# Attention and two feed-forward layers on one core: one ring of banks for the sums of the later blocks, two rings for their attention, scores due two pairs at a time

## The chip, the cores and the metric

The kernel runs on one core of a Trainium2 chip. The metric is device time in microseconds (us) of the whole kernel, as the median of the runs. The engines are named as the profile names them: PE (matrix products; PEld is its weight load), DVE (vector), ACT (scalar), POOL (GpSimd) and SP, whose queue starts most transfers.

## What is computed

```python
def reference(**kwargs):
    attn_out = _attn_ref(**attn_kwargs)      # q, k, v: (4, 8, 576, 64), causal window of 128, ALiBi bias
    x = attn_out.transpose(0, 2, 1, 3).reshape(B * S, H * D)   # 2304 tokens x 512
    x = _moe_ref(x=x, **moe_kwargs)          # h = x @ w_in (512 x 2048); g = gate(h); g @ w_out
    return _moe2_ref(x=x, **moe2_kwargs)

# _attn_ref
scores = scale * q @ k.T;  mask = (rel >= 0) & (rel < window)
scores = np.where(mask, scores + bias, -1e9)
attn = exp(scores - max) / (sum + 1e-09);  out = attn @ v
# _moe_ref
g = np.where(h >= 1, h, np.where(h <= -1, 0.0, (h + 1) ** 2 / 4))
# _moe2_ref: tokens with x @ w_skip > 0 also pass through one of 8 experts; the others are returned as they are
```

## The kernel before

The 2304 tokens are cut into 9 blocks of 256 (18 tiles of 128). A block needs attention for 4 pairs of heads and then 8 feed-forward steps, each over 256 of the 2048 hidden columns. fp32 operands of the feed-forward layers are split into a high and a low part, and three products stand for one, so a step is 24 matmuls of the first layer (L528, 128x256) and 12 of the second (L559, 128x512).

**Attention of one pair** (`pair`, L311 on). Load of q, k and v (L324, L327); q scaled (L334 on ACT, L336 on POOL); scores on PE in 64-row tiles, for the first blocks whole (L347: 4 instructions, 8 records) and for the later ones in halves on 64x64 tiles (L359: 8 instructions, 16 records); on DVE the merge of the halves (L376; whole: L370) and bias, row minimum and write to `sn` (L382); exp on ACT (L388); reciprocal of the row sums on DVE (L397, L398); normalisation (L416 on ACT, L419 on POOL); transposes on PE (L424); the copy to `pts` (L293); two masked selections into `ab` on POOL (L307); the product with v on PE in 128x64 tiles (L446: 6 instructions, 12 records); copy and rest into `xT` (L293, L302). `PLAN["whole"]` says how many blocks take whole scores.

**A feed-forward step** (`tile_ff`): first product (L528), `u` and its square on ACT (L540, L545), the gate on DVE (L550), high part on ACT (L293, `g<-h`), low part on DVE (L302, `g<-h,g`), second product (L559) into two accumulators of 128x512. The first three blocks run interleaved while the 32 weight tiles are being prepared (`weight`: ACT L474 and L293, DVE L480, L494, L499, L302); later blocks run one after the other. When a block is done, `evacuate` copies both sums out (ACT L293, `stage<-r`) and reduces them for the second layer's choice (DVE L574).

**PSUM.** There are eight banks in four rings of two: `h` for the first product, and `r0`, `r1`, `r2`, which `att` (scores, transposes, products with v) and `sums` (accumulators) hand out: block 0 sums in r0, block 1 in r1, block 2 in r2, later blocks in r2 and r1 by turns; attention takes r2 for the first three blocks and r0 afterwards.

**What sets the order.** No loop runs on the device: a planner (`Plan.order`) lays the pieces out on all five engines from costs, due times and buffer rings, and every engine executes its row in that order. `PLAN` holds its constants (`lead`: how far ahead of a block's first step its attention is due, and `spread`: how far apart the four pairs are), `ENGINES` the engines that each operation may choose from. Where the plan leaves PE idle early on, `run` inserts filler matmuls (L603) that no result depends on.

Of the kernel before, what the change touches and what calls it, by code (L numbers as in the profile page):

```python
# [22 lines left out]
P = 128  # L23
B, H, S, D = 4, 8, 576, 64
NT = B * S
DM = H * D
# [5 lines left out]
NPAIR = H // 2  # L32
# [12 lines left out]

PLAN = dict(base=4.418, d0=10.283, d1=3.632, d3=3, d2=5.432, lag=1, lag2=9, ahead=19.774, lead=22.491, spread=2,
            margin=1.2, slack=0.049, fin=0.449, passes=5, first=3, stick=4.711, zeros=0, whole=2)

ENGINES = dict(norm="AP", wlo="DP", rebias="A", pt="A", whi="A", square="A", scale="AP")

# [47 lines left out]
class Plan:  # L98
# [5 lines left out]
    def add(self, cost, fn, deps=(), new=(), use=(), due=1e9, lag=0.0, port=False,  # L104
            mode=""):
        p = Piece(len(self.pieces), cost, fn, [d for d in deps if d is not None], new, use, due, lag, port, mode)
        self.pieces.append(p)
        return p
# [129 lines left out]
dve = lambda n: n / 960.0 + 0.072  # L238
dve2 = lambda n: n / 1920.0 + 0.072
act = lambda n: n / 1200.0 + 0.108  # L240
actp = lambda n: n / 1200.0 + 0.068
# [4 lines left out]
class Fused:  # L246
# [23 lines left out]


    def bank(self, ring, shape):
        return self.buf(ring, 2, shape, psum=True)

    def att(self, g, shape):
        return self.bank("r2" if g < 3 else "r0", shape)

    def sums(self, g):
        return [self.bank(("r0", "r1", "r2")[g] if g < 3 else ("r2", "r1")[g % 2], [P, DM]) for _ in range(2)]

# [15 lines left out]

    def pick(self, key, **cost):
        return {e: cost[e] for e in ENGINES[key]}

# [12 lines left out]
    def pair(self, g, p, due):  # L312
        add, nc, a = self.plan.add, self.nc, self.a
# [4 lines left out]
        whole = g < PLAN["whole"]  # L318
        qk = self.buf("qkraw", 2, [P, 5, P])
        v = self.buf("vraw", 2, [P, 3, P])  # L320
        hd = slice(2 * p, 2 * p + 2)
        heads = [(odd, slice(64 * odd, 64 * odd + 64)) for odd in range(2)]
# [15 lines left out]

        lq = add(self.pick("scale", A=0.4, P=0.43, D=dve2(256)), scale, [lq], use=[qk], port=True)
        s = [self.att(g, [P, 2, 4, 64]) for _ in heads]  # L340

# [18 lines left out]

        sn = self.buf("sn", 2, [P, 4, P])
        sd = add({"T": (0.87 if g else 0.66) if whole else 0.63 if g else 0.5}, scores, [lq], new=s + [sn], use=[qk], mode="rows")
        st = self.buf("st", 4, [P, 2, 4])
        exps = []
        for odd, o in heads:
# [20 lines left out]
            def exp(e, odd=odd):  # L386
                for x in range(2 * odd, 2 * odd + 2):
# [3 lines left out]
            d = add({"D": dve(128 * (1 + j)) if whole else 2 * dve(64 * (1 + j)) + 0.06}, merge, [sd], use=[s[odd]])  # L391
            d = add({"D": 0.416}, rowmax, [d], new=[] if odd else [st],
                    use=[s[odd], sn, st])
# [8 lines left out]
        for odd, o in heads:  # L402
            pt = self.bank("r1", [P, 2, P]) if g < 2 else self.att(g, [P, 2, P])
            pts = self.buf("pts", 2, [P, 2, P])
# [21 lines left out]
            def before(e, pts=pts, ab=ab):  # L426
                if g == 0:
                    self.select(ab.t[:, 2:3, :], pts.t[:, 1:2, :], False)
                else:
                    self.select(ab.t[:, 0:4:2, :], pts.t, False)  # L430

            d = add(self.pick("norm", A=0.586, D=dve(256), P=0.67), norm, [rs], use=[sn, st], port=True)
            d = self.chain("tr", add({"T": 0.221}, transpose, [d], new=[pt, pts], use=[sn]))
            d = add(self.pick("pt", A=actp(256), D=dve(256)), lambda e, ptv=ptv, pts=pts: self.copy(e, pts.t, ptv()), [d],
                    use=[pt, pts])
            d1 = self.chain("ab", add({"P": pool1(256 if g else 128)}, before, [d], new=[ab], use=[pts]))
            last.append((o, ab, add({"P": pool1(256)}, lambda e, pts=pts, ab=ab: self.select(ab.t[:, 1:4:2, :], pts.t, True),
                                    [d, d1], use=[pts, ab])))
        av = self.att(g, [P, 2, P]) if g else self.bank("r0", [P, 2, P])

# [164 lines left out]
    def run(self):  # L605
# [12 lines left out]
        for g in range(NBLK):  # L618
            for p in range(NPAIR):
                self.pair(g, p, tau[pos[g, 0]] - c["lead"] - (NPAIR - 1 - p) * c["spread"] if g > 2 else 1e9)  # L620
        w = {}
# [215 lines left out]
```

## Time and profile before

| what | value |
|---|---|
| median of 3 runs | 527.0 us (526.81 to 528.45) |
| the profiled execution: device time | 527.1 us |
| its span, first to last instruction | 525.3 us |
| PE busy | 509.4 us, 97% of the span |
| ACT busy | 301.4 us, 57% |
| DVE busy | 277.2 us, 53% |
| POOL busy | 100.7 us, 19% |
| granted PE clock, mean | 0.995 |

Busy time is the time in which the profile shows an instruction on the engine. In a row of a timeline, the first number is the start in us from the span's beginning, the second the time from the first start to the last end; since matmuls overlap, what a group takes from PE is the distance from its start to the start of the next group. A wait in square brackets is idle time just before the group and what ended it.

### The profile page before, as it was taken

Reading aid. Unit: us, or ns where it says so; the run is one execution under the profiler, and the core shown is the slowest. Engines: PE = TensorE matmul, PEld = TensorE weight load, DVE = VectorE, ACT = ScalarE, POOL = GpSimd, SP = SyncE. Lnnn points to the kernel's source line nnn. Section 1 sums busy time; section 2 is a strip of 40 time slices with the busy share of each in tenths; the row PEclk is TensorE's granted clock in tenths of the full one; section 3 lists DMA queues with packets and bytes.
Section 4 is the critical chain, followed back from the end, with each engine's and each line's share of the span. In section 5 each row is a group of like instructions: output and inputs, shape, how many; then the busy total and the mean of one; then the engine's idle time right before and its main releaser. Section 6 shows DMA issues by size and latency. Waiting matters only on the chain.

```text
span 525.3 us, 10059 instructions
## 1 busy us (share of the span) xinstructions
PE 509.4 (97%) x3700; PEld 429.9 (82%) x3702; DVE 277.2 (53%) x844; ACT 301.4 (57%) x784; POOL 100.7 (19%) x244
## 2 busy tenths in 40 slices
PE   7999999999999999999999999999999999999994
PEld 3567898888888898889888988888888988889883
DVE  5989999998365225532555236422653265223221
ACT  6999778777477336643575237633763277433330
POOL 2673000234014200330033002400231013200000
PEclk9999999999999999999999999999999999999997
DMA  8565555553121202120212012210212020101001
GB/s 268 163 231 192 189 178 151 190 172 113 49 90 52 61 1 92 50 61 1 67 52 65 21 49 67 57 32 1 91 52 60 1 92 1 31 0 41 1 0 44
DMA packets 27141, 41.12 MB, mean 78 GB/s; under 512 B 2000, under 2 KB 15952, under 8 KB 27088
## 3 DMA queue, kind: packets, MB, share of 16 engines
q1 hardware_dynamic: 26416, 40.12, 24.2%
q8 instruction: 30, 0.49, 0.4%
q10 hardware_dynamic: 672, 0.33, 0.2%
q14 instruction: 23, 0.19, 0.1%
HBM read 35.72 MB, written 4.72 MB: 77 GB/s over the span
## 4 chain that ended last, share of the span: by engine, by line
PE 76%; DVE 11%; ACT 5%; DMA 3%; issue 2%; POOL 0%; SPq 0%; ACTq 0%; POOLq 0%; DVEq 0%
PE h L528 32%; PE r L559 32%; PE r L446 6%; PE r L359 4%; ACT sn L388 2%; PE r L424 2%; DVE stage L494 2%; DVE wtmp L499 2%; DVE r L376 2%; DMA qkraw<-in_qk 1%; DMA stage<-in_w_in 1%; DMA stage<-in_w_out 1%; DVE stage L480 1%; DVE sn L382 1%; ACT sn L416 1%
## 5 line engine op out<-in xcount | busy, mean ns | idle before, releaser
L528 PE MATMUL h<-xT,wi 128*128 128x256 f32 x1728 | 222.9, 282 | 0.6 <-POOL wi L302 0.4
L528 PEld LDWEIGHTS h<-xT,wi 128*128 128x128 f32 x1728 | 213.6, 188 | 11.7 <-issue 5.2
L559 PE MATMUL r<-wo,g 128*128 128x512 f32 x864 | 219.1, 400 | 0.0
L559 PEld LDWEIGHTS r<-wo,g 128*128 128x128 f32 x864 | 156.0, 188 | 37.7 <-issue 4.4
L550 DVE SCALAR_TENSOR_TENSOR h<-h,u 128x512 f32<-128x512 f32 x72 | 50.3, 698 | 129.3 <-ACT u L545 126.6
L540 ACT ACTIVATE u<-h,half 128x512 f32<-128x512 f32 x72 | 49.4, 686 | 111.1 <-PE h L528 110.5
L419 POOL TENSOR_SCALAR sn<-sn,st 128x128 f32<-128x128 f32 x70 | 27.1, 400 | 237.4 <-ACT u L540 175.7
L388 ACT ACTIVATE sn<-sn,st 128x128 f32<-128x128 f32 x144 | 56.1, 391 | 27.1 <-DVE st L382 27.0
L307 POOL TENSOR_SCALAR_AFFINE_SELECT ab<-pts 128x256 f32<-128x256 f32 (+1 forms) x144 | 56.5, 426 | 53.5 <-ACT pts L293 44.0
L293 ACT ACTIVATE g<-h 128x512 fp32r<-128x512 f32 x72 | 42.8, 594 | 33.1 <-DVE h L550 32.9
L302 DVE TENSOR_TENSOR g<-h,g 128x512 fp32r<-128x512 f32 x72 | 49.6, 689 | 22.2 <-ACT g L293 21.3
L545 ACT ACTIVATE u<-u 128x512 f32<-128x512 f32 x72 | 45.5, 632 | 1.4
L376 DVE COPY_PREDICATED r<-mask,r 64x128 f32<-64x128 uint8 x112 | 33.2, 296 | 15.9 <-PE r L359 12.9
L446 PE MATMUL r<-ab,vraw 128*64 128x128 f32 (+1 forms) x416 | 35.6, 315 | 3.5 <-ACT pts L293 1.7
L446 PEld LDWEIGHTS r<-ab,vraw 128*64 128x64 f32 x416 | 25.2, 136 | 14.6 <-issue 3.8
L382 DVE CUSTOM_DVE_ANT_0 sn<-r,nrel 128x128 f32<-128x128 f32 x144 | 33.3, 286 | 0.8
L574 DVE CUSTOM_DVE_ANT_0 junk<-r,wskip 128x512 f32<-128x512 f32 x18 | 12.4, 691 | 37.1 <-ACT stage L293 36.5
L388 ACT ACTIVATION_READ_ACCUMULATOR sn<-sn,st 128x1 f32 x144 | 27.0, 188 | 0.0
L416 ACT ACTIVATE sn<-sn,st 128x128 f32<-128x128 f32 x74 | 25.4, 394 | 1.7 <-DVE st L398 1.2
L424 PE MATMUL r<-ident,sn 128*128 128x128 f32 x144 | 23.7, 277 | 1.6 <-POOL sn L419 1.2
L474 ACT ACTIVATE wtmp<-stage 128x512 f32<-128x512 f32 x32 | 21.7, 679 | 5.3 <-DVE wi L302 2.2
L359 PE MATMUL r<-qkraw 64*64 64x192 f32 x448 | 24.7, 335 | 0.0
(43 smaller groups left out, 282.1 us busy)
## 6 DMA issues: line engine op xcount, KB each, us to landing
qkraw<-in_qk SPq DMA_DIRECT2D x32, 320.0 KB, 3.0
stage<-in_w_in SPq DMA_DIRECT2D x16, 512.0 KB, 3.6
stage<-in_w_out SPq DMA_DIRECT2D x16, 512.0 KB, 3.7
vraw<-in_v SPq DMA_DIRECT2D x32, 192.0 KB, 2.7
out_x<-stage SPq DMA_DIRECT2D x18, 256.0 KB, 2.0
qkraw<-in_qk SPq DMA_DIRECT2D x4, 256.0 KB, 4.2
vraw<-in_v SPq DMA_DIRECT2D x4, 128.0 KB, 4.2
nrel<-in_nrel ACTq DMA_DIRECT2D x1, 256.0 KB, 3.9
```

The source lines that it names most:

```text
L293: self.nc.scalar.activation(out=out, in_=in_, func=AF.Copy)
L302: eng.tensor_tensor(out=out, in0=in0, in1=in1, op=ALU.subtract)
L307: self.nc.gpsimd.affine_select(out=out, in_=in_, pattern=[[0, n], [sign, P]], compare_op=ALU.is_ge if causal else ALU.is_gt, fill=0.0, base=0,
L359: nc.tensor.matmul(s[odd].t[r, i, 1 - half:4 - half, :], qk.t[o, 3 + i, r], k, start=True, stop=True)
L376: nc.vector.copy_predicated(s.t[r, 1 - j:2, 1 + half, :], self.mask[r, 1 - j:2, r], s.t[r, 1 - j:2, 3 * (1 - half), :])
L388: nc.scalar.activation(out=sn.t[:, x, :], in_=sn.t[:, x, :], func=AF.Exp, scale=-1.0, bias=st.t[:, 0, x:x + 1], accum_out=st.t[:, 1, x:x + 1])
L446: nc.tensor.matmul(av.t[o, out, :], v.t[:, k, o], ab.t[:, m, :], start=not more, stop=True, skip_group_check=more)
L528: nc.tensor.matmul(h.t[:, c, :], w[:, wz, k, :], x.t[:, xz, k].rearrange("p a b -> p (a b)"), start=k == 0 and i == 0, stop=k == NKC - 1 a ...
L540: r = add({"A": 0.167 + 0.213 * n}, lambda e: nc.scalar.activation(out=uv(), in_=hv(), func=AF.Relu, scale=0.5, bias=self.half), [d], new= ...
L545: nc.scalar.activation(out=uv(), in_=uv(), func=AF.Square)
L550: r = add({"D": dve(256 * n)}, lambda e: nc.vector.scalar_tensor_tensor(out=hv(), in0=hv(), scalar=1.0, in1=uv(), op0=ALU.max, op1=ALU.min ...
L559: nc.tensor.matmul(acc[i].t, gt.t[:, gz, c, i * P:(i + 1) * P], self.wo[:, f, wz, :], start=f == 0 and j == 0, stop=f == NF - 1 and j == 2)
```

## The change

The accumulators of every block from block 3 on are taken from ring r1 alone. From block 4 on (`turn=4`) attention uses r0 for pairs 0 and 2 and r2 for pairs 1 and 3. The due time of the pairs comes in twos from block 4 on (`p | 1`). q and k get 4 buffers (2 before), v 3 (2), `sn` 3 (2). Block 2 has whole scores too (`whole=3`). In the later blocks the normalisation may go to DVE as well, the copy to `pts` to DVE or ACT; the first three blocks keep the choices that they had (keys ending in `0`). The low part of the weights is left to DVE alone, and for weight tile 0 one shift moves from DVE to a product on POOL (`zeros=1`). All other constants of the planner are new, and with them the order on every engine.

```diff
-PLAN = dict(base=4.418, d0=10.283, d1=3.632, ..., ahead=19.774, lead=22.491, spread=2, ..., zeros=0, whole=2)
-ENGINES = dict(norm="AP", wlo="DP", rebias="A", pt="A", whi="A", square="A", scale="AP")
+PLAN = dict(base=2.305, d0=10.296, d1=4.965, ..., ahead=15, lead=50.043, spread=7.771, ..., zeros=1, whole=3, turn=4)
+ENGINES = dict(norm="ADP", wlo="D", rebias="A", pt="AD", whi="A", square="A", scale="AP", norm0="AP", pt0="A",
+               scale0="AP")
...
-    def att(self, g, shape):
-        return self.bank("r2" if g < 3 else "r0", shape)
+    def att(self, g, p, shape):
+        return self.bank("r2" if g < 3 or g >= PLAN["turn"] and p % 2 else "r0", shape)
 
     def sums(self, g):
-        return [self.bank(("r0", "r1", "r2")[g] if g < 3 else ("r2", "r1")[g % 2], [P, DM]) for _ in range(2)]
+        return [self.bank(("r0", "r1", "r2")[g] if g < 3 else "r1", [P, DM]) for _ in range(2)]
...
-    def pick(self, key, **cost):
+    def pick(self, key, g=9, **cost):
+        if g < 3:
+            key += "0"
         return {e: cost[e] for e in ENGINES[key]}
...
-        qk = self.buf("qkraw", 2, [P, 5, P])
-        v = self.buf("vraw", 2, [P, 3, P])
+        qk = self.buf("qkraw", 4, [P, 5, P])
+        v = self.buf("vraw", 3, [P, 3, P])
...
-        sn = self.buf("sn", 2, [P, 4, P])
+        sn = self.buf("sn", 3, [P, 4, P])
...
-                self.pair(g, p, tau[pos[g, 0]] - c["lead"] - (NPAIR - 1 - p) * c["spread"] if g > 2 else 1e9)
+                self.pair(g, p, tau[pos[g, 0]] - c["lead"] - (NPAIR - 1 - (p if g < c["turn"] else p | 1)) * c["spread"]
+                          if g > 2 else 1e9)
```

In the order that comes out, PE's lines move by four (L359 is L363, L424 is L428, L446 is L450, L528 is L532, L559 is L563). Counted over the whole order, PE goes to scores 36 times before and 27 times now: the 24 pairs of blocks 3 to 8 had 24 such visits and have 15, since nine times the scores of two pairs stand next to one another, and the four pairs of block 2 have whole scores. It goes to the product with v 21 times before and 26 times now. There are 36 filler matmuls before and 38 now.

**PE, from a pair's last transposes to the products with v, in a later block.** Before (block 5; `r` is a bank of a ring, x12 and x24 are matmuls of the first feed-forward product):

```order
L559 MATMUL r_2599<-wo,g 128x512 x6
L424 MATMUL r_2797<-ident,sn 128x128 x2
L424 MATMUL r_2801<-ident,sn 128x128 x2
L528 MATMUL h<-xT,wi 128x256 x12
L446 MATMUL r_2830<-ab,vraw 64x256 x2
L446 MATMUL r_2830<-ab,vraw 64x128 x4
L446 MATMUL r_2837<-ab,vraw 64x256 x2
L446 MATMUL r_2837<-ab,vraw 64x128 x4
```

Now:

```order
L428 MATMUL r_3185<-ident,sn 128x128 x2
L428 MATMUL r_3190<-ident,sn 128x128 x2
L563 MATMUL r_2712<-wo,g 128x512 x6
L532 MATMUL h<-xT,wi 128x256 x24
L450 MATMUL r_3236<-ab,vraw 64x256 x2
L450 MATMUL r_3236<-ab,vraw 64x128 x4
L450 MATMUL r_3246<-ab,vraw 64x256 x2
L450 MATMUL r_3246<-ab,vraw 64x128 x4
```

Between the transposes and the products that need them stand 12 matmuls of the first layer before, and 6 of the second with 24 of the first now.

**DVE, from the last row minimum of a visit to the low part of g, in a later block.** Before:

```order
L382 ISA st_3991 128x1
L550 SCALAR_TENSOR_TENSOR h_3912<-h_3912,u_3974 128x512
L397 TENSOR_SCALAR st_3991<-st_3991 128x4
L398 RECIPROCAL st_3991<-st_3991 128x4
L302 TENSOR_TENSOR g_4015<-h_3912,g_4015 128x512
```

Now (numbers behind the names tell buffers apart):

```order
L386 ISA st_4006 128x1
L554 SCALAR_TENSOR_TENSOR h_3927<-h_3927,u_4002 128x512
L401 TENSOR_SCALAR st_3992<-st_3992 128x4
L402 RECIPROCAL st_3992<-st_3992 128x4
L415 TENSOR_TENSOR sn_3948<-sn_3948,st_3992 128x256 x2
L401 TENSOR_SCALAR st_4006<-st_4006 128x4
L402 RECIPROCAL st_4006<-st_4006 128x4
L415 TENSOR_TENSOR sn_3959<-sn_3959,st_4006 128x256
L306 TENSOR_TENSOR g_4059<-h_3927,g_4059 128x512
```

Ahead of the first row stand the merges and row minima of one pair before (two rows of x2 merges and 4 minima) and of two pairs now (four rows of x2 and 8 minima); behind the gate, the low part of g now also stands behind two reciprocals and three normalisations.

**ACT, the first instructions of the program after its table load and two transfers.** Before:

```order
L334 ACTIVATE qkraw_110<-qkraw_110,qscale_87 128x256
L334 ACTIVATE qkraw_112<-qkraw_112,qscale_87 128x256
L474 ACTIVATE wtmp_142<-stage_114 128x512
L388 ACTIVATE sn_129,st_139<-sn_129,st_139 128x128 x4
L474 ACTIVATE wtmp_174<-stage_135 128x512
L388 ACTIVATE sn_155,st_167<-sn_155,st_167 128x128 x4
```

Now:

```order
L338 ACTIVATE qkraw_110<-qkraw_110,qscale_87 128x256
L338 ACTIVATE qkraw_112<-qkraw_112,qscale_87 128x256
L338 ACTIVATE qkraw_114<-qkraw_114,qscale_87 128x256
L338 ACTIVATE qkraw_116<-qkraw_116,qscale_87 128x256
L392 ACTIVATE sn_129,st_142<-sn_129,st_142 128x128 x4
L478 ACTIVATE wtmp_169<-stage_118 128x512
L392 ACTIVATE sn_156,st_171<-sn_156,st_171 128x128 x4
```

All four pairs of block 0 are scaled on ACT, the first exps no longer stand behind a weight tile, and on SP's queue four loads of q and k (two before) stand ahead of the first weight tile.

## Rows read from the trace of the kernel before

**Rows 1.** The page's part 1, PE: busy us (share of the span) xinstructions.

```profile
PE 509.4 (97%) x3700; PEld 429.9 (82%) x3702; DVE 277.2 (53%) x844; ACT 301.4 (57%) x784; POOL 100.7 (19%) x244
```

**Rows 2.** Busy time in stretches, as headed: start, weights, first and last full block.

```profile
core 0: us, PE busy (x) PEld busy (x) DVE busy (x) ACT busy (x) POOL busy (x), PEclk, DMA share, GB/s
10.00:40.00 30.00, 27.47 (x194) 17.73 (x198) 25.44 (x103) 29.28 (x109) 21.50 (x47) 1.00 0.63 199
...
50.00:125.00 75.00, 74.81 (x522) 65.31 (x520) 73.14 (x160) 57.70 (x123) 12.30 (x21) 1.00 0.54 178
...
146.39:201.58 55.19, 54.99 (x417) 47.18 (x416) 23.87 (x81) 29.26 (x79) 10.26 (x27) 1.00 0.16 49
...
367.74:423.01 55.27, 54.99 (x417) 47.19 (x416) 23.72 (x81) 29.14 (x79) 10.27 (x27) 1.00 0.16 48
```

**Rows 3.** Timeline of PE in one later block: start, us, instructions [idle before].

```profile
143.59 2.96 PE L559 MATMUL r<-wo,g 128*128 128x512 f32 x12
146.49 0.88 PE L359 MATMUL r<-qkraw 64*64 64x192 f32 x16
147.30 3.09 PE L528 MATMUL h<-xT,wi 128*128 128x256 f32 x24
150.32 0.88 PE L359 MATMUL r<-qkraw 64*64 64x192 f32 x16
151.13 3.06 PE L559 MATMUL r<-wo,g 128*128 128x512 f32 x12
154.03 2.99 PE L528 MATMUL h<-xT,wi 128*128 128x256 f32 x24
...
168.48 1.66 PE L528 MATMUL h<-xT,wi 128*128 128x256 f32 x12
170.35 1.96 PE L446 MATMUL r<-ab,vraw 128*64 128x256 f32 x24 [0.20 <-ACT pts L293]
172.24 1.68 PE L528 MATMUL h<-xT,wi 128*128 128x256 f32 x12
...
181.90 2.96 PE L559 MATMUL r<-wo,g 128*128 128x512 f32 x12
184.71 2.99 PE L528 MATMUL h<-xT,wi 128*128 128x256 f32 x24
187.53 2.96 PE L559 MATMUL r<-wo,g 128*128 128x512 f32 x12
```

**Rows 4.** The last eight and the last four records of the visit at 146.49.

```profile
146.86 0.51 PE L359 MATMUL r<-qkraw 64*64 64x192 f32 x8
...
147.03 0.34 PE L359 MATMUL r<-qkraw 64*64 64x192 f32 x4
```

**Rows 5.** Timeline of PE in the start: whole scores, one pair's product with v.

```profile
28.78 1.13 PE L347 MATMUL r<-qkraw 64*128 64x256 f32 x8
29.84 2.03 PE L528 MATMUL h<-xT,wi 128*128 128x256 f32 x15
...
35.42 1.09 PE L446 MATMUL r<-ab,vraw 128*64 128x256 f32 x12 [0.83 <-DVE st L382]
36.44 0.44 PE L424 MATMUL r<-ident,sn 128*128 128x128 f32 x2
```

**Rows 6.** PE's waits from 60 us on: us in total, times, longest us.

```profile
PE r L446 <- ACT pts L293: 1.7, 5, 0.7
```

**Rows 7.** Timeline of DVE: the start of one pair's merges, and the gate behind its minima.

```profile
262.06 1.28 DVE L376 COPY_PREDICATED r<-mask,r 64x128 f32<-64x128 uint8 x4
...
264.35 0.70 DVE L550 SCALAR_TENSOR_TENSOR h<-h,u 128x512 f32<-128x512 f32 x1
```

**Rows 8.** Timeline of ACT, first weight tile and first two exps.

```profile
7.50 0.69 ACT L474 ACTIVATE wtmp<-stage 128x512 f32<-128x512 f32 x1 [1.30 <-DMA stage<-in_w_in]
8.10 0.39 ACT L388 ACTIVATE sn<-sn,st 128x128 f32<-128x128 f32 x1
...
8.48 0.38 ACT L388 ACTIVATE sn<-sn,st 128x128 f32<-128x128 f32 x1
```

More of the change, by code (lines that the diff above doesn't have):

```diff
@@ L38 @@
 SCRATCH = 1024
-PLAN = dict(base=4.418, d0=10.283, d1=3.632, d3=3, d2=5.432, lag=1, lag2=9, ahead=19.774, lead=22.491, spread=2,
-            margin=1.2, slack=0.049, fin=0.449, passes=5, first=3, stick=4.711, zeros=0, whole=2)
-ENGINES = dict(norm="AP", wlo="DP", rebias="A", pt="A", whi="A", square="A", scale="AP")
+PLAN = dict(base=2.305, d0=10.296, d1=4.965, d3=3.352, d2=5.226, lag=1, lag2=8, ahead=15, lead=50.043, spread=7.771,
+            margin=1.2, slack=0.019, fin=0.206, passes=5, first=3, stick=5.562, zeros=1, whole=3, turn=4)
+ENGINES = dict(norm="ADP", wlo="D", rebias="A", pt="AD", whi="A", square="A", scale="AP", norm0="AP", pt0="A",
+               scale0="AP")
 WARM = dict(start=2.2, end=40.0, room=0.2, each=0.3)
@@ L337, in scale @@
                                                                      scalar2=1.0, op0=ALU.mult, op1=ALU.mult)
-        lq = add(self.pick("scale", A=0.4, P=0.43, D=dve2(256)), scale, [lq], use=[qk], port=True)
-        s = [self.att(g, [P, 2, 4, 64]) for _ in heads]
+        lq = add(self.pick("scale", g, A=0.4, P=0.43, D=dve2(256)), scale, [lq], use=[qk], port=True)
+        s = [self.att(g, p, [P, 2, 4, 64]) for _ in heads]
         def scores(e):
@@ L402, in pair @@
         for odd, o in heads:
-            pt = self.bank("r1", [P, 2, P]) if g < 2 else self.att(g, [P, 2, P])
+            pt = self.bank("r1", [P, 2, P]) if g < 2 else self.att(g, p, [P, 2, P])
             pts = self.buf("pts", 2, [P, 2, P])
@@ L430, in before @@
                     self.select(ab.t[:, 0:4:2, :], pts.t, False)
-            d = add(self.pick("norm", A=0.586, D=dve(256), P=0.67), norm, [rs], use=[sn, st], port=True)
+            d = add(self.pick("norm", g, A=0.586, D=dve(256), P=0.67), norm, [rs], use=[sn, st], port=True)
             d = self.chain("tr", add({"T": 0.221}, transpose, [d], new=[pt, pts], use=[sn]))
-            d = add(self.pick("pt", A=actp(256), D=dve(256)), lambda e, ptv=ptv, pts=pts: self.copy(e, pts.t, ptv()), [d],
+            d = add(self.pick("pt", g, A=actp(256), D=dve(256)), lambda e, ptv=ptv, pts=pts: self.copy(e, pts.t, ptv()), [d],
                     use=[pt, pts])
@@ L438, in pair @@
                                     [d, d1], use=[pts, ab])))
-        av = self.att(g, [P, 2, P]) if g else self.bank("r0", [P, 2, P])
+        av = self.att(g, p, [P, 2, P]) if g else self.bank("r0", [P, 2, P])
         def avs(e):
```

## The prediction

> **What bounds the kernel now.** I read the page's busy shares first: PE is busy 509.4 of 525.3 us, the next engine, ACT, 57% [rows 1]. Then the stretches: in the later blocks PE is busy 54.99 of 55.2 us per block, with ACT near 29, DVE near 24 and the granted clock at 1.00, which is the upper of its two levels, 2.4 GHz [rows 2]. So from about 50 us on the time is the sum of what stands in PE's row plus a few waits. Earlier two other engines are full: ACT, 29.28 of 30 us between 10 and 40 us, and DVE, 73.14 of 75 us between 50 and 125 us, while PE is full there too [rows 2]. So a change can pay in three ways: less in PE's row, fewer waits in the later blocks, or an earlier end of the start. The feed-forward matmuls are the same in number; 24 of the first product take 2.82 us and 12 of the second 2.81 us, start to start [rows 3].
>
> **Visits to scores.** From 143.59 to 154.03 us there are two visits to scores, 24 matmuls of the second product and 24 of the first. 10.44 - 2 x 2.81 - 2.82 = 2.00, so a lone visit costs 1.00 us [rows 3]. Its own start-to-start time is only 0.81 (146.49 to 147.30); the other 0.19 is lost going in and coming out. Within the visit four records go off together, and the next four 0.16 to 0.17 us later [rows 4]. A second pair that follows in the same visit therefore costs 4 x 0.165 = 0.66 and saves 0.34. The order does this nine times: -3.1. If the change of pair costs as much as a new visit the saving is 0; if it costs only the own 0.81, 9 x 0.19 = -1.7 is left. I take -3.1, since the four rows within a visit are the nearest thing to a second pair.
>
> **Whole scores in block 2.** 1.06 us start to start instead of 0.81 [rows 5, 3], four pairs: +1.0. DVE has two merges less per pair there; it is full then, but this is below 2 us spread over a time in which PE does not wait, and I cost it at nothing.
>
> **Visits to the product with v.** 24 records for two pairs take 1.89 us (170.35 to 172.24), 12 for one pair 1.02 (35.42 to 36.44) [rows 3, 5]. One visit split in two costs 2 x 1.02 - 1.89 = 0.15 and once more the 0.19 of going in and out: 0.34. Five more visits: +1.7. In one place more than before a visit to scores stands directly beside one to the product with v, which by the same 0.19 is worth -0.2. Together the visits give -3.1 + 1.0 + 1.7 - 0.2 = -0.6.
>
> The Trainium skill's page "TensorEngine Tiling (Array Packing)", section "Key Properties", says that a change of the tiling mode drains TensorE, not merely a change of tile. The 0.19 around each visit agrees with that. By the page the two visits that stand beside one another would still pay, since their modes differ, and the visits would give -0.4; two pairs' scores share a mode, so the -3.1 would stay.
>
> **Waits in the later blocks.** Each block's first products with v follow the transposes of the last pair needed by only 12 matmuls of the first layer, and PE waits for ACT's copy to `pts`: 1.7 us in five waits, the longest 0.7 [rows 6]. One reads 0.20 where start to start 168.48 to 170.35 is 1.87 [rows 3], a little more than idle, matmuls and entry make. I take 2.0 for all six blocks. Now 6 matmuls of the second product and 24 of the first stand between, 1.4 + 2.82 = 4.2 us, so these waits go: -2.0. What comes late next is the second product behind the merged visit, for which see the next part.
>
> **The row on DVE that grows.** One pair's merges and minima take DVE from 262.06 to 264.35, 2.29 us, before the gate of the step can start [rows 7]. Two pairs take 4.6. At the start of a block PE's row is: scores of two pairs, 12 matmuls of the first product that complete a step, 12 of the second product of the step before, 24 of the first, then this step's second product. From the step's end that leaves 2.81 + 2.82 = 5.6 us, and some 0.5 more until the low part of g is read. DVE starts its 4.6 us when the first pair's scores are there, 0.66 + 0.1 + 1.41 = 2.2 us before the step ends, so the gate starts 2.4 us after it; ACT has 8 exps of 0.38 [rows 8], 3 us, in its row ahead of g's high part, and DVE two reciprocals and three normalisations ahead of g's low part. That adds up to 5.5 to 6.3 us: just enough, or 0.2 short. In the other merged visit of a block a visit to the product with v (1.89) stands in between as well, so nothing is late. The trace of before has no such row; bounds are 0 and 9 x 0.4 = 3.6; I take +0.7 (five places at 0.15).
>
> **The crowded stretch.** With `lead` at 50 instead of 22 us blocks 4 and 5 get their scores early, and in the two steps after block 2's end four pairs are merged and normalised. On DVE that is 4 x 2.29 = 9.2 us [rows 7] and two gates with their low parts (about 2.8), copies and normalisations, some 15 us in about 16.5 us of PE's row; ACT has 16 exps (6.1 us [rows 8]) and likewise about 15. Before, a block had 24 and 29 us in 55 [rows 2]. Bounds: 0, and 2.5 if PE waits for one pair's full 2.29 there; I take +0.7. That the normalisation may go to DVE takes work from ACT, which is what makes these 15 us fit. More buffers for q, k, v and `sn` remove no wait that the trace shows on PE; they let scores start early, and alone I cost them at nothing. Sums in r1 alone: between a block's last second product and the next block's first stand 12 matmuls, the merged scores and 12 matmuls, 1.41 + 1.85 + 1.41 = 4.7 us, against two copies on ACT and two reductions on DVE of 0.6 to 0.7 each, which stand directly behind the sums in both rows: at nothing. Cover gone (the exps ahead of a copy), it would be up to 1 per block.
>
> **The start.** ACT is the full engine. It now scales four pairs first and starts exps without the weight tile that waited 1.30 us for its transfer [rows 8]: at best -1.3. Against it, the first weight tile's load stands behind two more loads, and POOL and ACT do as much as before; the nearest row for a late load is that same wait of 1.30, and for two loads I bound it at half as much again, +1.9; and the order has two more fillers than before (38), which says that the plan too sees no less idle time there. I take -0.5, bounds -1.3 and +1.9. The three weight tiles whose low part moves from POOL to DVE add 2 us to a full DVE, about what the merges and the shift take off it: nothing.
>
> **Sum.** -0.6 - 2.0 + 0.7 + 0.7 - 0.5 = -1.7 on a span of 525.3, which is 523.6. The profiled execution took 527.1, its span lies 1.8 below that, and the median of the runs is 527.0; so 527.0 - 1.7 = **525.3 us**.
>
> **Rivals.**
> First, a larger gain: the start gives its 1.3, DVE's longer row and the crowded stretch cost nothing: -0.6 - 2.0 - 1.3 = -3.9, some 523.1 us. For it speaks that ACT bounds the start and its first exps stood behind a transfer; against it the fillers.
> Second, the gain is given back: start 0 to +1, crowded stretch +1.5: 527.0 us. For it speaks that both engines are nearly full in that stretch, against it that such an order was laid out with these costs in view and that the trace of before shows few waits anywhere.
> Third, slower: DVE's row of two pairs holds up the gate and with it the second product in each of the nine merged visits. With 0.65 us more at each, 5.9 instead of 0.7, the time is 530.5. It decides from 0.45 us per visit on, which is where the gains are gone and 1.6 us more with them. It needs the room of 5.6 to 6.1 us to be missed by a good deal, also where a visit to the product with v lies in between; that speaks against it.
> Fourth, the visits do not save, since a change of pair costs like a new visit (-3.1 becomes 0): 528.4 at most, and with the -1.7 of the middle bound 526.7.
>
> **How the numbers follow.** Forecast 0.42 (its own range 524.0 to 526.6), larger gain 0.25, given back 0.20, slower 0.10, no saving by visits 0.03. A measurement of this kernel can tell about 0.3%, 1.6 us, from no change: faster means below 525.4, slower above 528.6. Faster: 0.25 and 0.6 of the forecast's 0.42, together 0.50. Same: the other 0.17, 0.20 and 0.03, together 0.40. Slower: 0.10. The range that should hold 8 in 10 leaves out the slower case and the far end of the larger gain: 522.4 to 528.0.
>
> **What would show it.** Right: PE's distance from one score visit with 32 records to the next group near 1.47; no wait for `pts` ahead of L450 in blocks 6 to 8; PE idle below 0.3 us per late block; the first exp near 7.2 us. Wrong: idle time of PE ahead of L563 released by DVE (low part of g) behind merged visits, which is the third rival; idle time between 180 and 230 us, or a first L563 much later than 47 us, which is the second; and a 32-record visit of 1.6 or more, which is the fourth. The sum is most at risk in the start, whose terms I can bound but not add up.

## The result, and the profile after

The changed kernel takes 521.6 us in the median of 4 runs (521.24 to 522.55), beside 526.9 for the kernel before; the ratio is 0.9908 with a 95% interval of 0.9888 to 0.9928. A second series gave 521.4 us and 0.9903 (0.9888 to 0.9918). That is 5.3 and 5.6 us less than the kernel before in the same series, where 1.7 less had been forecast, and 521.6 lies below the stated range.

The profiled execution took 522.55 us, its span is 520.8, 4.5 less than before. The page's first part, beside [rows 1]:

```profile
PE 511.4 (98%) x3669; PEld 433.2 (83%) x3672; DVE 289.9 (56%) x879; ACT 287.8 (55%) x741; POOL 96.4 (19%) x221
```

Work moved from ACT (13.6 us less) to DVE (12.7 more), as the order says. PE is busy 2.0 us longer in a span that is 4.5 shorter, so what went is its idle time, and it is still what bounds the kernel. The first two stretches of [rows 2] again, and 55 us in the middle, about one block:

```profile
core 0: us, PE busy (x) PEld busy (x) DVE busy (x) ACT busy (x) POOL busy (x), PEclk, DMA share, GB/s
10.00:40.00 30.00, 28.96 (x181) 17.89 (x183) 26.04 (x111) 28.05 (x104) 24.33 (x48) 1.00 0.68 228
50.00:125.00 75.00, 75.00 (x490) 65.83 (x490) 71.98 (x157) 57.97 (x122) 7.79 (x15) 1.00 0.53 178
...
290.00:345.00 55.00, 55.00 (x433) 47.94 (x426) 26.86 (x90) 26.82 (x72) 8.87 (x22) 1.00 0.16 49
```

PE has no idle time left in this late stretch (55.00 of 55.00) nor in the stretch in which the weights are prepared (75.00 of 75.00, where [rows 2] has 74.81). The waits of PE from 60 us on, in the columns of [rows 6] and, like there, without the 1.7 us ahead of the program's last small product, which are the same before and after: the wait for the copy to `pts` is gone, and one wait stands in the crowded stretch, at 213.58.

```profile
PE r L450 <- DVE st L386: 0.6, 1, 0.6
```

**Where the 4.5 us are.** Three places can be read directly. The last block's last 36 matmuls of the second product start at 509.06 before and at 506.94 now, 2.12 earlier. The last reduction on DVE, from which the program decides whether the experts run, starts at 519.59 and 517.47, again 2.12 apart. The spans end at 525.29 and 520.84: from the last reduction to the end it takes 5.70 before and 3.37 now. So 2.3 of the 4.5 us lie behind the last visible instruction. Timelines of PE and DVE, before and after:

```profile
509.06 8.56 PE L559 MATMUL r<-wo,g 128*128 128x512 f32 x36
...
519.59 0.17 DVE L669 TENSOR_REDUCE toti<-tot 1x1 int32<-1x18 f32 x1 [0.39 <-PE tot L667]
```

```profile
506.94 8.56 PE L563 MATMUL r<-wo,g 128*128 128x512 f32 x36
...
517.47 0.16 DVE L674 TENSOR_REDUCE toti<-tot 1x1 int32<-1x18 f32 x1 [0.39 <-PE tot L672]
```

What follows there is the jump over the experts' code (L671 before, L676 now), which all engines take, and the engines' meeting at the program's end. In the records of before DVE has its last semaphore instruction at 521.00 and its next one, the drain at the end, at 524.41; all the other engines have drained by 522.21 and wait. After the change the two stand at 518.89 and 519.00.

**How the rest of PE's row is split.** For the other 2.1 us each group of PE's row gets its price from the steady blocks ([rows 3 to 5]: 0.1176 us per first product, 0.2334 per second, visits as in the prediction), and the sum up to a group is subtracted from that group's start. What remains is the time lost up to there: waits, a slower PE, and the filler matmuls, which have no price. Up to the last 36 second products the row before is worth 487.8 us at these prices, the row now 487.1. The time lost, in us, for two executions of the row before and three of the row now (the 30 and 75 idle writes of two of them, told of below, stand in the last blocks):

| lost up to | before | before, 30 idle writes | after | after again | after, 75 idle writes |
|---|---|---|---|---|---|
| 45 us | 17.8 | 18.2 | 17.9 | 16.7 | 16.1 |
| 126 us | 19.1 | 19.3 | 18.5 | 16.7 | 16.1 |
| 235 us | 19.7 | 19.7 | 19.6 | 17.8 | 17.3 |
| the last 36 second products | 21.3 | 20.8 | 19.8 | 18.0 | 17.5 |

So by the means of the columns the order now loses 1.1 us less up to 45 us, 1.0 less from 45 to 126, 0.6 more from 126 to 235 and 1.1 less after that, and its work is 0.7 shorter: together 3.3, and with the 2.3 at the end 5.6, beside 5.3 and 5.6 in the medians. The three executions of the changed row differ by 1.8 us at 45 us, so the 1.1 up to there is rough. The profile shown first is the longest of the four runs of the changed kernel, and it lost most in the first 15 us.

### The profile page after: what moved, and what is told of

Read it like the earlier page. It is cut to its first block, busy times and chain, and to the rows that moved or that the text cites. A ratio compares the mean times of both kernels' runs of the same rounds, so it can differ in the third digit from the quotient of the medians.

```text
span 520.8 us, 9925 instructions
## 1 busy us (share of the span) xinstructions
PE 511.4 (98%) x3669; PEld 433.2 (83%) x3672; DVE 289.9 (56%) x879; ACT 287.8 (55%) x741; POOL 96.4 (19%) x221
## 4 chain that ended last, share of the span: by engine, by line
PE 92%; ACT 3%; DVE 2%; DMA 1%; issue 1%; POOL 0%; SPq 0%; ACTq 0%
PE r L563 39%; PE h L532 39%; PE r L450 6%; PE r L363 3%; PE r L428 3%; PE r L351 2%; ACT sn L392 1%; DMA stage<-in_w_out 1%; DMA qkraw<-in_qk 1%; DVE sn L386 1%; ACT pts L295 0%; PE h L607 0%; DVE r L380 0%; DVE r L374 0%; DVE wtmp L503 0%
## 5 line engine op out<-in xcount | busy, mean ns | idle before, releaser
L532 PEld LDWEIGHTS h<-xT,wi 128*128 128x128 f32 x1728 | 214.7, 188 | 11.7 <-issue 4.4
L532 PE MATMUL h<-xT,wi 128*128 128x256 f32 x1728 | 223.8, 282 | 0.1
L563 PE MATMUL r<-wo,g 128*128 128x512 f32 x864 | 219.2, 398 | 0.0
L563 PEld LDWEIGHTS r<-wo,g 128*128 128x128 f32 x864 | 155.4, 188 | 34.9 <-issue 3.3
L311 POOL TENSOR_SCALAR_AFFINE_SELECT ab<-pts 128x256 f32<-128x256 f32 (+1 forms) x144 | 59.4, 445 | 151.9 <-ACT pts L295 142.8
L392 ACT ACTIVATE sn<-sn,st 128x128 f32<-128x128 f32 x144 | 56.0, 391 | 11.2 <-DVE st L386 10.9
L450 PE MATMUL r<-ab,vraw 128*64 128x128 f32 (+1 forms) x416 | 38.2, 316 | 1.3 <-POOL ab L311 0.6
L380 DVE COPY_PREDICATED r<-mask,r 64x128 f32<-64x128 uint8 x96 | 28.4, 296 | 16.7 <-PE r L363 14.0
L450 PEld LDWEIGHTS r<-ab,vraw 128*64 128x64 f32 x416 | 25.9, 136 | 13.9 <-issue 3.7
L340 POOL TENSOR_SCALAR qkraw<-qkraw,qscale 128x256 f32<-128x256 f32 x24 | 13.1, 545 | 127.0 <-DMA qkraw<-in_qk 121.9
L295 ACT ACTIVATE pts<-r 128x256 f32<-128x256 f32 x53 | 19.2, 378 | 19.0 <-PE r L428 18.9
L423 POOL TENSOR_SCALAR sn<-sn,st 128x128 f32<-128x128 f32 x46 | 22.0, 491 | 33.2 <-DVE st L402 24.2
L428 PE MATMUL r<-ident,sn 128*128 128x128 f32 x144 | 24.2, 276 | 0.0
L503 DVE SCALAR_TENSOR_TENSOR wtmp<-wtmp,stage 128x512 int32<-128x512 int32 x32 | 21.9, 691 | 0.3 <-ACT wtmp L478 0.2
```

What stands on the lines that cost most here:

```text
L295: self.nc.scalar.activation(out=out, in_=in_, func=AF.Copy)
L311: self.nc.gpsimd.affine_select(out=out, in_=in_, pattern=[[0, n], [sign, P]], compare_op=ALU.is_ge if causal else ALU.is_gt, fill=0.0, base=0,
L392: nc.scalar.activation(out=sn.t[:, x, :], in_=sn.t[:, x, :], func=AF.Exp, scale=-1.0, bias=st.t[:, 0, x:x + 1], accum_out=st.t[:, 1, x:x + 1])
L428: nc.tensor.transpose(ptv()[:, i, :], sn.t[:, 2 * odd + i, :], self.ident)
L450: nc.tensor.matmul(av.t[o, out, :], v.t[:, k, o], ab.t[:, m, :], start=not more, stop=True, skip_group_check=more)
L532: nc.tensor.matmul(h.t[:, c, :], w[:, wz, k, :], x.t[:, xz, k].rearrange("p a b -> p (a b)"), start=k == 0 and i == 0, stop=k == NKC - 1 a ...
```

## Experiments

**1. The end.** The theory: DVE's jump must wait for code, depending on where the jump stands in its row. Writes of one column that nobody reads were put into DVE's row in the last blocks, where it is mostly idle (the lines for 30 of them; 75 come five at a time):

```diff
+        self.spare = c.tile([P, 1], F32, tag="spare", name="spare")
+        self.pads = 30
...
                 p.fn(e)
+                if e == "D" and t > 440:
+                    for _ in range(min(2, self.pads)):
+                        self.nc.vector.memset(self.spare, 0.0)
+                        self.pads -= 1
```

> The kernel before with 30 idle writes more on DVE, one column each, spread over the last blocks, where DVE is idle. Theory A (the end): in the trace of before DVE's last instruction comes 3.4 us after its jump over the second layer's experts, and one more load of code is seen there than after the change; where the jump stands in DVE's row decides, so 30 instructions more bring the end from 5.7 us after the last reduction (L669) down to about 3.4, and the time from 526.9 to about 524.6. Theory B (chance): the 3.4 us belong to that one execution and not to the program; then the time stays at 526.9, within 0.5.

> The changed kernel with 75 idle writes more on DVE in the last blocks. DVE executed 53 instructions more than before; with 75 more the jump stands 128 further than in the kernel before, and the code on DVE is loaded in pieces of 8 KB, 128 instructions. Theory A: the end takes 5.7 us again, and the time rises by 2.3, from 521.6 to about 523.9. Theory B: no change, 521.6 within 0.5.

> The changed kernel with 30 idle writes more on DVE. Theory A with the piece counted from the load: the piece that holds the jump's target was loaded when DVE entered the piece of the jump, so nothing waits and the time stays at 521.6. Theory A with the jump's own piece: a target outside that piece must be loaded again, and the time is 523.9. Theory B: 521.6.

> The changed kernel once more, unchanged, as the neighbour of the others: 521.6 within 0.5, the end again 3.3 us from the last reduction to the end of the span, and PE's row up to the last small product (L672) at 517.2 or up to 1 less, since three of the four runs so far were about 1 us shorter than the profiled one.

The end did what theory A says: 3.39 us from the reduction on for the kernel before with 30 writes (5.70 without), 5.14 for the changed one with 75, 3.37 with 30, which is the first of the two forms that theory A had there. But the times were 527.3, 526.5 and 524.2, and the unchanged neighbour's 521.4: what was won at the end of the first was lost elsewhere, and the other two were slower by far more than the end. PE's row against its twin without writes showed a loss that grew evenly from 60 us on, long before the first idle write, by 0.5 to 0.6 us per 100 us. The new tile of one column takes 32 bytes a partition, and all tiles laid behind it in memory had moved by 32 bytes, `xT` among them, which the first product reads.

**2. The end again, with no tile moved.** The idle writes now go to a second column of the tile `one`, which has room for it:

```diff
-        one = skp.tile([P, 1], F32, tag="one", name="one")
+        both = skp.tile([P, 2], F32, tag="one", name="one")
+        one = both[:, 0:1]
...
+            f.spare, f.pads = both[:, 1:2], 30
```

> The kernel before with the 30 idle writes on DVE in its last blocks again, now into a tile that is there already, so that no tile moves in memory. Theory A (DVE's jump waits for its code): the end goes from 5.7 to 3.4 us and the time from 527.0 to 524.7. In the first attempt the end did shorten by 2.3, but every first product (L528) took 1.5% longer from 50 us on, well ahead of the idle writes. Theory C (place): that came from the new tile of 32 bytes, which put xT on addresses that are no multiple of 64; then the first product takes 119.2 ns from start to start here, as in the kernel before. Theory D (the writes themselves slow PE): 121.4 ns again, and the time stays at 527.

> The changed kernel with 75 idle writes on DVE into a tile that is there already. Theory A: the end takes 5.1 to 5.7 us instead of 3.4, and the time rises from 521.4 by 1.8 to 2.3, to 523.2 to 523.7. Theory C: 119.1 ns per first product from start to start, as in the changed kernel. Chance as the cause of the longer end: 521.4.

The kernel before with 30 idle writes takes 524.3 us, a ratio of 0.9951 (0.9936 to 0.9967): 2.5 us for 30 instructions that do nothing. The changed kernel with 75 of them takes 524.35 (0.9951, 0.9934 to 0.9968), 2.9 more than without. The end takes 3.38 and 5.28 us. In the second kernel that is 1.9 of the 2.9 us; where the other 1.0 lies is open, since the profiled execution is the shortest of its seven (522.2 to 525.8). From one first product to the next PE takes 117.6 and 117.8 ns by the mean from 50 us on, as in the two kernels without writes (117.6 and 117.7); with the tile of 32 bytes it was 119.8 and 119.7. (The expectations' figures are read in another way and lie some 1.5 ns higher; the difference of about 2 ns is the same.) So theory C holds, and of theory A what it says of the place of the jump: the idle writes shorten the end of the one kernel and lengthen that of the other.

The views of the transfers between the last reduction and the end of the span, 40 slices of equal length, before and then before with 30 idle writes:

```profile
GB/s 417 173 0 0 0 0 0 0 0 0 0 0 115 172 57 0 0 0 0 0 0 0 0 0 0 0 0 0 0 0 0 0 0 0 0 0 0 0 57 0
...
q14 instruction: 5, 0.04, 2.4%
```

```profile
GB/s 387 387 194 24 0 0 0 0 0 0 0 0 0 0 0 0 0 0 0 0 0 193 193 97 97 0 0 0 0 0 0 0 0 0 0 0 0 0 0 0
...
q14 instruction: 4, 0.03, 3.0%
```

In the first line code comes in about 1.8 us after the reduction, then nothing moves for some 3 us, and one more piece of code comes shortly before the end. In the second line the code is the last thing that moves. All kernels of this study, by the instructions that DVE had executed when it came to the jump:

```
instructions of DVE before the jump | from the last reduction to the end, us
 948  before          5.70      1005  two_whole       3.35
 955  start_only      5.57      1015  no_pairs        3.35
 976  before_pad30    3.39      1030  after_pad30     3.37
 976  before_30idle   3.38      1035  old_lead        3.35
 976  rest_only       3.35      1075  after_75idle    5.28
1001  after           3.37      1075  after_pad75     5.14
1001  shift64         3.37
```

Long ends at 948, 955 and 1075, short ones from 976 to 1035. In each long end DVE alone is late, by 2.0 to 3.3 us against the short ones, but not at the same instruction: in start_only at the first behind the jump (4.55 us after the reduction, beside 1.4 in the others), in the kernel before at the second (the drain at 524.41), in both kernels with 75 writes at the third (4.93 and 4.79, beside 2.8). In the kernel before 950 instructions of DVE stand ahead of the one that is late, in the two with 75 writes 1078, which is 128 more, and DVE's code arrives in pieces of 8192 bytes. So the standstill belongs to a place in DVE's code that comes back after 128 instructions. That DVE waits there for code is inferred from this, not shown: the late piece in the first line starts 5.46 us after the reduction, 0.6 us after DVE has gone on, and in the 2 us before that no transfer is seen. The Trainium skill's page "Runtime: NRT & Kernel Launch", section "Instruction fetch mechanics", says that a taken branch whose target is outside the pages held must fetch the target's page before the engine goes on. The standstill directly behind the jump in start_only agrees with it; in the other long ends DVE executes one or two instructions behind the jump first. The page gives no price, and here the standstill makes the end 1.8 to 2.3 us longer.

**3. Where the tiles lie.** The loss of the first attempt asked whether multiples of 64 bytes matter, or of more. Only one line is added to the changed kernel:

```diff
+        c.tile([P, 16], F32, tag="gap", name="gap")
```

> The changed kernel with an unused tile of 64 bytes a partition ahead of the working tiles, so that xT lies on multiples of 128 bytes instead of 64 above one. Nothing else differs. If only multiples of 64 matter: 521.4 and 119.1 ns per first product. If multiples of 128 help further: about 118 ns, 1728 x 1 ns = 1.7 us less, 519.7. If any move costs: 524, as with the tile of 32 bytes.

522.8 us, a ratio of 0.9917 (0.9902 to 0.9933): 1.4 more than the kernel without it, whose interval (0.9888 to 0.9918) overlaps this one. Timelines of PE in the late blocks, one step each: the changed kernel again, with its tiles moved by 32 bytes, and by 64.

```profile
440.41 2.99 PE L532 MATMUL h<-xT,wi 128*128 128x256 f32 x24
443.23 2.96 PE L563 MATMUL r<-wo,g 128*128 128x512 f32 x12
```

```profile
448.47 3.03 PE L534 MATMUL h<-xT,wi 128*128 128x256 f32 x24
451.34 0.86 PE L565 MATMUL r<-wo,g 128*128 128x512 f32 x3
```

```profile
438.31 3.04 PE L533 MATMUL h<-xT,wi 128*128 128x256 f32 x24
441.19 2.95 PE L564 MATMUL r<-wo,g 128*128 128x512 f32 x12
```

The 24 first products take 2.82, 2.87 and 2.88 us from start to start; over all of them from 50 us on the mean of one is 117.7, 119.7 and 119.1 ns. From 240 us on PE's row loses 1.1 us by the move of 64 bytes, beside its twin. The profiled execution is the longest of its six (524.6) and lost more in the start as well, where the granted clock stood at 0.51 for 3.4 us behind a wait of 2.0 us; so it does not say where the rest of the 1.4 lies. A place on a multiple of 128 bytes is no better for the first product than the one in the kernel as it stands, which is the best of the three. Why is open; none of the three expectations was met.

**4. Pairs one by one again.**

```diff
-                self.pair(g, p, tau[pos[g, 0]] - c["lead"] - (NPAIR - 1 - (p if g < c["turn"] else p | 1)) * c["spread"]
+                self.pair(g, p, tau[pos[g, 0]] - c["lead"] - (NPAIR - 1 - p) * c["spread"]
```

> The changed kernel with the due times of the pairs one by one again (p in place of p | 1). In the order that comes out the scores of blocks 3 to 8 take 22 visits instead of 15, with 2 merged ones instead of 9, and the product with v 34 visits instead of 26. By the prices of the prediction (0.34 per visit): 7 x 0.34 + 8 x 0.34 = 5.1 us more on PE's row, 526.5. If a change of pair costs as much as a new visit, only 2.7 more: 524.1. If the visits are hidden in other waits: 521.4.

529.9 us, a ratio of 1.0057 (1.0036 to 1.0079): 3.4 more than the highest of the three expectations. The whole time grows by more than the visits, since the planner lays the start anew as well. The steady blocks can be compared by themselves: the period from one product with v to the next of its kind, here, and in the changed kernel.

```profile
345.11 1.09 PE L450 MATMUL r<-ab,vraw 128*64 128x256 f32 x12 [0.30 <-DVE st L386]
...
400.71 1.09 PE L450 MATMUL r<-ab,vraw 128*64 128x256 f32 x12 [0.30 <-DVE st L386]
```

```profile
312.01 1.96 PE L450 MATMUL r<-ab,vraw 128*64 128x256 f32 x24
...
366.28 1.96 PE L450 MATMUL r<-ab,vraw 128*64 128x256 f32 x24
```

55.60 and 54.27 us a block: 1.33 more. Two merged visits to scores and two joint ones to the product with v become four and four, and 4 x 0.34 = 1.36 by the prediction's prices. That the two agree is partly luck: the block here has a wait of 0.30 for DVE in it, which the other has not, and without it 1.03 are left, 0.26 a visit; several of these visits stand beside one another and share a way in and out. At the prediction's prices PE's whole row up to the last 36 second products is 4.8 us longer, beside 5.1 expected; the other 4 to 6 us are lost time (19.5 instead of 16.9 at 45 us, and 23.9 instead of 18.4 at the end). So the visits are not hidden, and a change of pair within a visit costs less than a new visit.

**5. The change in two halves.** One kernel has only the new constants of the start, the other all the rest.

```diff
-base=4.418, d0=10.283, d1=3.632, d3=3, ..., lag2=9, ahead=19.774, ..., slack=0.049, fin=0.449, ..., stick=4.711, zeros=0
+base=2.305, d0=10.296, d1=4.965, d3=3.352, ..., lag2=8, ahead=15, ..., slack=0.019, fin=0.206, ..., stick=5.562, zeros=1
-wlo="DP"
+wlo="D"
```

These lines make start_only of the kernel before; the same lines the other way round make rest_only of the changed kernel.

> The kernel before with the changed kernel's constants of the start alone (pace of the steps of the first three blocks, zeros=1, the low part of the weights on DVE); rings, whole scores, due times of the pairs and engines of the later blocks as before. In the profiles so far PE's row reached 126 us with 0.6 to 3 us less lost after the change. If the constants of the start bring that, this kernel gains 0.6 to 3 us: 524 to 526.2, with the later blocks 55.1 to 55.7 us each and the end at 5.7, since DVE has only one instruction more than before. If the gain at the start comes from the whole scores of block 2, the rings or the later due times, the time stays at 526.8.

> The changed kernel with the constants of the start of the kernel before: the complement of the run above. Later blocks 54.3 us each as after the change, so -0.7 for the visits and about -1.5 for the waits; the end short if DVE's 20 instructions more are enough (-2.3). If the start is where the rest of the gain is: about 526.8 - 0.7 - 1.5 - 2.3 = 522.3, and 1 to 2 us slower than the changed kernel. If the start has no part in it: 521.4, like the changed kernel.

530.3 us (1.0073, 1.0055 to 1.0092) and 526.8 (0.9998, 0.9987 to 1.0009): neither half is faster than the kernel before, both expectations missed. The first loses 24.0 us up to 126 us, in four waits of PE for DVE's low part of g and others for DVE; the second loses 22.4, and 20.3 of it up to 45 us, while its late blocks (54.27 us) and its end are those of the changed kernel, as expected. The gain of the start shows in neither half alone. But the first half's late blocks are of use: 54.92 us each (339.72 to 394.64) with the rings and due times of before and with no wait at all. So the waits for `pts` go by another order alone; and from 54.92 to the changed kernel's 54.27 it is 0.65 a block, two merged visits at 0.33.

**6. Single constants** of the changed kernel, in two_whole and in old_lead.

```diff
-whole=3
+whole=2
```

```diff
-lead=50.043
+lead=22.491
```

> The changed kernel with whole=2: block 2's four pairs in halves again. By the prediction's prices whole scores cost 0.25 us each on PE's row, so this kernel should take 1.0 us less, 520.4. If the two merges saved per pair on DVE, which is full up to 126 us, are worth more than that, it is slower: with 4 x 2 x 0.3 = 2.4 us more on DVE, 521.4 - 1.0 + 2.4 = 522.8.

> The changed kernel with lead at 22.491 as before. The crowded stretch from 208 to 214 us, in which PE lost 0.9 us (0.6 of it on a row minimum of DVE), comes from blocks 4 and 5 having their scores early. If that is so the stretch empties and the time falls by 0.5 to 0.9, to 520.5 to 520.9. If an early lead is what keeps the later blocks free of waits for the copy to pts, these come back: up to 2 us more, 523.4.

528.9 us (1.0041, 1.0029 to 1.0054) and 528.3 (1.0029, 1.0011 to 1.0046), 6.1 and 4.9 us above the highest that was expected of each. PE's row is 1.4 and 0.5 us shorter than that of the changed kernel by the prices, and the late blocks run at the same 54.27. Both lose it where DVE is full, up to 126 us: two_whole has lost 25.7 us by then, old_lead 25.2. In two_whole it is one wait. The waits of PE, its timeline around that wait, and the stretches:

```profile
PE r L563 <- ACT g L295: 3.7, 2, 3.5
```

```profile
99.70 0.88 PE L363 MATMUL r<-qkraw 64*64 64x192 f32 x16
104.04 5.53 PE L563 MATMUL r<-wo,g 128*128 128x512 f32 x12 [3.46 <-ACT g L295]
109.37 0.78 PE L428 MATMUL r<-ident,sn 128*128 128x128 f32 x4
```

```profile
100.00:103.00 3.00, 0.58 (x16) 0.22 (x8) 2.74 (x7) 1.89 (x4) 0.00 (x0) 0.99 0.83 279
103.00:106.00 3.00, 1.96 (x5) 1.38 (x6) 3.00 (x7) 1.79 (x3) 0.00 (x0) 0.50 0.32 127
106.00:109.70 3.70, 3.70 (x11) 2.85 (x10) 3.70 (x14) 2.17 (x9) 0.00 (x0) 0.50 0.50 143
```

PE waits 3.5 us; within this wait the granted clock falls to 0.50, the lower of the two levels (1.2 GHz), and the 12 second products that follow take 5.33 us (104.04 to 109.37) instead of 2.81. One wait cost 6 us. old_lead has such a place at 83 us, behind a wait of 3.1 us for DVE's low part of g.

So the crowded stretch could not be tested by itself: what the early lead costs at 208 to 214 us, 0.9, is small beside what the other order loses at 83.

## Why the prediction was wrong

**The end: the step that is missing.** The prediction takes the time from the last second product to the end as the same before and after, and never prices it. It was 5.70 us from the last reduction and is 3.37. The row for it was there: in the trace of before PE, DVE and ACT have nothing to do for the last 5.5 us, and the transfers show loads of code in them. The idle writes show that the place of DVE's jump sets this time: 30 of them make the kernel before 2.5 us faster. The change adds 53 instructions to DVE's row ahead of the jump for reasons of its own, so this gain is luck. It accounts for 2.3 of the 3.7 us by which the forecast was short; with it the forecast would have been 523.0, inside the stated range. The terms found, in the order of the parts below: -0.7, -1.1, 0, +0.6 and -2.1, and with the -2.3 of the end -5.6.

**The visits: right.** -0.6 forecast, -0.7 found (487.8 to 487.1). A visit for two pairs was to take 1.47 us from start to start; the timeline of PE in the changed kernel has 1.46:

```profile
268.17 1.57 PE L532 MATMUL h<-xT,wi 128*128 128x256 f32 x12
269.67 1.53 PE L363 MATMUL r<-qkraw 64*64 64x192 f32 x32
271.13 1.68 PE L532 MATMUL h<-xT,wi 128*128 128x256 f32 x12
272.65 2.96 PE L563 MATMUL r<-wo,g 128*128 128x512 f32 x12
```

From 268.17 to 275.45 there are 24 first products, 12 second ones and the visit: 7.28 - 2.82 - 2.81 = 1.65, where a lone one costs 1.00. The second pair costs 0.65; 0.66 was taken. The fourth rival falls. Where a visit to the product with v and one to scores stand side by side, from 213.58 to 215.41, they take 1.02 and 0.81, their own times, with nothing in between, which bears out the -0.2. The 1.85 that the prediction gives merged scores between two blocks is 1.66 by its own prices; no term of the sum hangs on it.

**The late waits: right in the mechanism, smaller in size.** The waits for `pts` went, but -2.0 was what one execution of before showed; the second lost 1.1 instead of 1.6 us from 235 us on, and 0.2 are still lost now. The means give 1.1 less there.

**DVE's row of two pairs: the working was right, the price was not.** +0.7 was taken for five places; no wait of PE ahead of L563 is found. The steps can be followed behind the visit at 269.67, in the timelines of DVE and PE:

```profile
270.60 2.60 DVE L380 COPY_PREDICATED r<-mask,r 64x128 f32<-64x128 uint8 x8 [0.91 <-PE r L363]
...
275.05 0.70 DVE L554 SCALAR_TENSOR_TENSOR h<-h,u 128x512 f32<-128x512 f32 x1
...
278.08 0.68 DVE L306 TENSOR_TENSOR g<-h,g 128x512 fp32r<-128x512 f32 x1
```

```profile
275.45 2.99 PE L532 MATMUL h<-xT,wi 128*128 128x256 f32 x24
278.28 2.96 PE L563 MATMUL r<-wo,g 128*128 128x512 f32 x12
```

The step ends at 272.65, the gate starts 2.4 us later, as worked out, and the low part of g is there at 278.76, 6.1 us after the step's end; 5.5 to 6.3 were worked out, with room for 5.6 to 6.1. PE starts at 278.28 with the high part and does not wait. There was no room to spare, and yet the third rival, in which DVE's row holds PE up, did not come.

**The crowded stretch: right.** +0.7 was taken; the order loses 0.3 at 160 us and 0.9 at 208 to 214, and 0.6 more than before from 126 to 235 by the means.

**The start: mis-sized, and its cause open.** -0.5 was taken for everything up to 126 us. By the means it is -2.1: 1.1 up to 45 us, within the bounds that were given, and 1.0 from 45 to 126, where the prediction put nothing, since DVE is as full as before (71.98 of 75 us). The gain that the prediction saw at the beginning did not come in its form. The first exp was to start near 7.2 us; in the three executions of the changed row it starts at 7.91, 8.09 and 7.92, beside 8.10 and 8.47 in two of the row before. The weight tile no longer stands ahead of it, but four scalings do, and they wait for the loads of q and k. Timeline of ACT in the changed kernel:

```profile
6.03 0.51 ACT L338 ACTIVATE qkraw<-qkraw,qscale 128x256 f32<-128x256 f32 x1 [0.99 <-DMA qkraw<-in_qk]
6.84 0.51 ACT L338 ACTIVATE qkraw<-qkraw,qscale 128x256 f32<-128x256 f32 x1 [0.30 <-DMA qkraw<-in_qk]
7.50 0.51 ACT L338 ACTIVATE qkraw<-qkraw,qscale 128x256 f32<-128x256 f32 x1 [0.16 <-DVE st L386]
7.91 0.39 ACT L392 ACTIVATE sn<-sn,st 128x128 f32<-128x128 f32 x1
```

From 45 to 126 us the order of before lost 1.1 to 1.3, most of it in three places of 0.2 to 0.4 that the view of the waits names in part only. The second execution of before shows them too, so they are of its order. Which edit removes them stays open: the two halves lose more there than either kernel.

**The first rival**, 523.1, came nearest in PE's row: by the means the row ends 3.3 us earlier, so without the end the time would be 523.7, between the forecast and that rival. As the rival has it, DVE's longer row cost nothing; the crowded stretch did cost 0.6.

## What to carry to other kernels

Account for the whole span before the changed part is priced: the stretch behind the last visible instruction too, above all where the program jumps; there an edit that only changes how many instructions an engine has was worth 2.5 us here, and it must be told apart from what the edit was made for. Where work is laid out by a planner, compare the steady blocks by their period and the start by the time lost, since any one constant lays everything anew. An experiment that adds a tile moves the others: add to a tile that is there.

## What the runs showed of the hardware

**The place of a jump.** 1.8 to 2.3 us at the end of the program hang on where DVE's jump stands: long at 948, 955 and 1075 instructions, short at 976 to 1035. The instruction that is late has 950 instructions ahead of it in one kernel and 1078 in two others, 128 apart. The other engines take the same jump and show no such wait in these traces.

**Addresses and the first product.** Moving the working tiles by 32 or 64 bytes made a first product 1.7 and 1.2% longer by the mean (117.7 to 119.7 and 119.1 ns from one to the next). With 32 bytes the changed kernel took 2.8 us longer, with 64 its blocks from 240 us on 1.1. No rule for it follows from three places.

**A wait can cost twice.** In waits of 3.1 us (old_lead) and 3.5 us (two_whole) the granted clock fell to 0.50 and stayed there for 3.4 and 6.8 us. Also the start of one and the same order differs by up to 1.8 us at 45 us from one execution to another, and PE's pace with it: the same two fillers take 1.04 us in one and 0.60 in another, on PE's timelines of the changed kernel without and with the 75 late writes.

```profile
5.09 1.65 PE L351 MATMUL r<-qkraw 64*128 64x128 f32 x8 [0.76 <-ACT qkraw L338]
6.67 1.04 PE L607 MATMUL h<-wskip 128*128 128x512 bf16 x2
7.95 1.93 PE L351 MATMUL r<-qkraw 64*128 64x128 f32 x8 [0.24 <-DVE st L386]
```

```profile
4.49 1.49 PE L351 MATMUL r<-qkraw 64*128 64x128 f32 x8 [0.16 <-ACT qkraw L338]
5.92 0.60 PE L607 MATMUL h<-wskip 128*128 128x512 bf16 x2
7.19 1.20 PE L351 MATMUL r<-qkraw 64*128 64x128 f32 x8 [0.67 <-DVE st L386]
```

The next fillers, four in a row, take 1.89 and 1.04 us, so each one more takes 0.43 and 0.22, close to the ratio of the two clock levels, though the view of the stretches gives 1.00 for the first 14 us of the first: its record of the granted clock begins at 14.3 us, that of the other at 5.7, and the pace is the full one from there on. So a difference of 1 or 2 us in the first 45 us of a single profile says little of an order.
